# k'v for two heads as one whole-array matmul, and the later chunks' attention at full depth in one bank, in a fused linear-attention and two-layer-expert kernel

## The chip, the cores and the metric

The kernel runs as one launch on one core of a Trainium2 chip. The metric is the device time of that launch in microseconds (us); each kernel is run several times and the median is taken. Beside the timed runs there is one profiled execution, from which every row below comes.

## The reference

Three stages follow each other. A linear attention without softmax over 8 batches, 8 heads, 576 positions and a head width of 64; a dense two-layer network with a leaky activation over the 4608 tokens; and a second network in which each token goes to the one of 8 experts that its gate picks.

```python
kv = np.einsum('bhsd,bhse->bhde', k, v)
out = np.einsum('bhsd,bhde->bhse', q, kv)
rms = np.sqrt(np.mean(out * out, axis=-1, keepdims=True) + 1e-06)
x = out / rms * g_norm                      # transposed, then reshaped to (4608, 512)
h = x @ w_in
x = (np.maximum(h, 0.0) + alpha * np.minimum(h, 0.0)) @ w_out
e = argmax(x @ w_gate + modality_bias[modality_id])       # one expert for a token
out[mask_e] = gate * (np.maximum(x[mask_e] @ w1[e], 0.0) @ w2[e])
```

The change touches the first two lines alone: `kv`, a 64x64 matrix for each batch and head, and `out`, the product of q with it.

## The kernel before

The work falls into a start (the first chunk's attention, some 22 us), a loop over 12 chunks of 384 tokens (to about 883 us), and the experts after it. The instructions stand in the order in which the program is written; no planner moves them, and each engine takes its own in that order.

In the loop, a chunk `c` runs through 16 steps `s`. A step is `first(c, s)`, 12 matmuls of 384 columns (L372), then `second(c, s-1)`, 9 matmuls of 512 columns (L393), both on numbers that are split in a high and a low part. ScalarE (`A`, rows ACT), VectorE (`V`, DVE) and GpSimd (`G`, POOL) prepare the operands of `second` from what `first` gave (L374, L375, L379, L381), and VectorE computes the gate's dot products of the chunk before (L410). TensorE (`PE`) has 21 matmuls in a step, and beside them, at some steps, the attention of the chunk that comes next.

Heads are worked on in pairs: pair `p` of 4 stands for two heads, with k and v of both side by side in the 256 columns of a tile `kvt`: columns 0 to 63 and 64 to 127 hold k of the two heads, 128 to 191 and 192 to 255 hold v. The positions, 576 of them, are five slices of up to 128 rows.

- `kv_mm(b, p)`, at steps 3 and 7 of those chunks in which a new batch begins (two pairs each time), multiplies for each slice and each of the two heads 64 columns of k with 64 columns of v (L229). The result for head 0 lies on partitions 0 to 63, that for head 1 on 64 to 127 of a bank `kvps`, each in columns of its own.
- `kv_evict(b)` copies these two quarters into `kvbd[b % 2]`, whose other two quarters stay at zero from the start: for each pair `p` it is a 128x128 matrix with the two heads' matrices on its diagonal.
- `attend(c, ts)`, at step 8 for two tiles of 128 tokens and at step 10 for one, multiplies q with it (L246). A matmul takes 32 tokens of one head: 64 rows deep, 32 columns of weights (q is the stationary operand), 64 columns of output. The four pairs of heads go to partitions 0, 32, 64 and 96 and the two heads of a pair to two banks `ps[0]` and `ps[1]`.
- `attended(c, t)`, at steps 8, 9 and 10, copies each of the two banks into `xs` (L256) and squares each into `junk` (L257), in strides that put the heads side by side again. VectorE then sums the squares (L289).

The first batch and the first chunk don't go this way: `kv_pair` (L265) and `attend_pair` (L271) do the same product with whole-array matmuls of 128 rows, 128 columns of weights and 128 columns of output, and f32 operands as well. `warm` (L824) keeps TensorE busy at the start with transposes of a 128x128 tile.

The banks that `attend` and `kv_mm` write come from a pool of two (`ps_a`, through `other()`), so an allocation waits until the one before the last has been read. Every f32 matmul shows in the trace as two passes, each a record of a weight load (engine PEld) and one of a matmul (PE); the split matmuls of L372 and L393 show as one.

Of the kernel before, what the change touches and what calls it, by code (L numbers as in the profile page):

```python
# [15 lines left out]
AF = mybir.ActivationFunctionType  # L16
# [7 lines left out]
S = 576  # L24
E = 8
NB = 8
CT = 384
# [21 lines left out]
def fused(ctx: ExitStack, tc, qT, kv, g2, wmoe, alpha, wgate, bias, modality, w12, out):  # L49
    nc = tc.nc  # L50
    V, A, G, PE, SP = nc.vector, nc.scalar, nc.gpsimd, nc.tensor, nc.sync
# [36 lines left out]
    kvbd = [one.tile([128, 4, 128], F32, name=f"kvbd{i}") for i in range(2)]  # L88
    xs = one.tile([128, 3, D], F32, name="xs")
    xhi = one.tile([128, 4, CT], F32R, name="xhi")  # L90
    xlo = one.tile([128, 4, CT], F32R, name="xlo")
    junk = one.tile([128, D], F32, name="junk")
# [7 lines left out]
    q_t, kv_t, raw_t, cut_t, g_t, xt_t, y_t, ms_t, sp_t = {}, {}, {}, {}, {}, {}, {}, {}, {}  # L100
    lg_t, kvps, hot_t, tps_t, pos_t, sq_t, rsqrt_t, yb_t = {}, {}, {}, {}, {}, {}, {}, {}
    ops, ops_t = [], {}
# [4 lines left out]
    def other(n=512):  # L107
        return (pools[1] if pools else ps_a).tile([128, n], F32, tag="a", name="a")
# [114 lines left out]
    def kv_mm(b, p):  # L223
        if p == 0:
            kvps[b] = four(other())
        t = kv_t.pop((b, p))
        for s in range(5):
            for o in (0, 64):
                PE.matmul(kvps[b][o:o + 64, p, o:o + 64], t[:, s, o:o + 64], t[:, s, 128 + o:192 + o], start=(s == 0), stop=(s == 4))  # L229

    def kv_evict(b):
        ps = kvps.pop(b)
# [2 lines left out]

    def attend(c, ts):

        q = q_t[c]
        ps = [other(256 * len(ts)).rearrange("p (a b) -> p a b", b=64) for _ in range(2)]
        for a in range(4 * len(ts)):  # L240
            o = ts[0] * 128 + 32 * a
            kvs = kvbd[(c * CT + o) // S % 2]
            for p in range(4):
                for h in range(2):
                    r = slice(64 * h, 64 * h + 64)
                    PE.matmul(ps[h][32 * p:32 * p + 32, a, :], q[r, p, o:o + 32], kvs[r, p, r], start=True, stop=True)  # L246
        for i, t in enumerate(ts):
            ops_t[c, t] = [p[:, 4 * i:4 * i + 4, :] for p in ps]

    def attended(c, t):  # L250
        ps = ops_t.pop((c, t))
        x = xs[:, t, :].rearrange("p (a h b) -> p a h b", a=4, h=2)
        sq = junk.rearrange("p (a h b) -> p a h b", a=4, h=2)
        xt_t[c, t] = xs[:, t, :].rearrange("p (a b) -> p a b", b=64)
        for h in range(2):
            A.copy(x[:, :, h, :], ps[h])  # L256
            A.activation(sq[:, :, h, :], ps[h], AF.Square)  # L257

    def kv_pair(p):

# [537 lines left out]
    with tc.manual_schedule():  # L798
# [71 lines left out]
        for c in range(NCH):  # L870
# [3 lines left out]
            for s in range(NFB):  # L874
# [55 lines left out]
                if kvb and s in (3, 7):  # L930
                    kv_mm(kvb[0], s - 3 and 2)
                    kv_mm(kvb[0], (s - 3 and 2) + 1)
# [8 lines left out]
                if nxt < NCH:  # L941
                    at = AT if c == 0 else 8
                    if at < s <= at + 3:
                        squares(nxt, s - at - 1)
                    if at <= s < at + 3:
                        if s != at + 1:
                            attend(nxt, (0, 1) if s == at else (2,))
                        attended(nxt, s - at)
                    if s == 11 and nxt + 1 < NCH:
                        load_q(nxt + 1)  # L950
                    if c == 0 and s in (at + 4, at + 5):
                        rsqrt(nxt, later, s - at - 4)
                    if c == 0 and s == at + 5:
                        scale_x(nxt, 0)
                    if c == 0 and s == at + 6:
                        scale_x(nxt, 1)
                        turn_x(nxt, 0)
                        scale_x(nxt, 2)
                        turn_x(nxt, 1)
                        turn_x(nxt, 2)  # L960
                    if c > 0 and s == at + 3:
                        rsqrt(nxt)
                    if c > 0 and s == at + 4:
                        scale_x(nxt, 0)
                        scale_x(nxt, 1)
                        turn_x(nxt, 0)
                    if c > 0 and s == at + 5:
                        scale_x(nxt, 2)
                        turn_x(nxt, 1)
                        turn_x(nxt, 2)  # L970
# [34 lines left out]
        c = NCH - 1  # L1005
# [109 lines left out]
```

## Time and profile before

| what | us |
|---|---|
| median of 3 runs | 1352.28 (1351.08 to 1353.52) |
| the profiled execution's own time | 1351.64 |
| its span, first to last instruction | 1350.0 |
| PE busy | 1335.8 (99%) |
| PEld busy | 1149.8 (85%) |
| DVE busy | 978.3 (72%) |
| POOL busy | 643.9 (48%) |
| ACT busy | 606.6 (45%) |

The profiled execution is 0.64 us below the median of the runs. Busy times are sums over the whole span, in which records of one engine that overlap count once. A matmul's record lasts longer than the time until the next one may begin, so what one costs is read from start to start. The granted clock of TensorE is at its full level (2.4 GHz) in all 40 slices of the page.

### The profile page before, as it was taken

Reading aid. Unit: us, or ns where it says so; the run is one execution under the profiler, and the core shown is the slowest. Engines: PE = TensorE matmul, PEld = TensorE weight load, DVE = VectorE, ACT = ScalarE, POOL = GpSimd, SP = SyncE. Lnnn points to the kernel's source line nnn. Section 1 sums busy time; section 2 is a strip of 40 time slices with the busy share of each in tenths; the row PEclk is TensorE's granted clock in tenths of the full one; section 3 lists DMA queues with packets and bytes.
Section 4 is the critical chain, followed back from the end, with each engine's and each line's share of the span. In section 5 each row is a group of like instructions: output and inputs, shape, how many; then the busy total and the mean of one; then the engine's idle time right before and its main releaser. Section 6 shows DMA issues by size and latency. Waiting matters only on the chain. (4 is left out here: it accounts for less than half of the span.)

```text
span 1350.0 us, 26562 instructions
## 1 busy us (share of the span) xinstructions
PE 1335.8 (99%) x8856; PEld 1149.8 (85%) x8856; DVE 978.3 (72%) x2041; ACT 606.6 (45%) x1329; POOL 643.9 (48%) x647
## 2 busy tenths in 40 slices
PE   8999999999999999999999999999999999999997
PEld 7888888889888889888888988878888888888886
DVE  5779686877877686969596969576766666666664
ACT  4763443443434343443434343254544444444444
POOL 4866464554645454645464555453333333333321
PEclk9999999999999999999999999999999999999999
DMA  8956556452646463546564443557411271637784
GB/s 302 325 191 198 200 195 205 166 195 100 206 153 209 161 207 128 180 166 216 167 212 153 141 165 126 202 189 264 150 48 47 63 279 48 265 102 294 302 320 187
DMA packets 84340, 250.68 MB, mean 186 GB/s; under 512 B 13101, under 2 KB 34605, under 8 KB 82032
## 3 DMA queue, kind: packets, MB, share of 16 engines
q1 hardware_dynamic: 72448, 220.82, 46.1%
q0 software_dynamic: 11760, 28.14, 6.4%
q8 instruction: 78, 1.28, 0.4%
q14 instruction: 54, 0.44, 0.1%
HBM read 158.69 MB, written 91.54 MB: 185 GB/s over the span
## 5 line engine op out<-in xcount | busy, mean ns | idle before, releaser
L372 PE MATMUL h<-xhi,W 128*128 128x384 f32 x1536 | 428.8, 341 | 0.2 <-POOL W L186 0.2
L381 POOL TENSOR_TENSOR glo<-gg,ghi 128x384 fp32r<-128x384 f32 x192 | 202.9, 1057 | 365.7 <-ACT ghi L379 321.4
L410 DVE CUSTOM_DVE_ANT_0 junk<-yrow,wg_sb 128x512 f32<-128x512 f32 x242 | 305.9, 1264 | 9.5 <-ACT yrow L404 4.0
L393 PE MATMUL y<-W,ghi 128*128 128x512 f32 x1152 | 299.7, 395 | 1.4 <-ACT ghi L379 1.0
L372 PEld LDWEIGHTS h<-xhi,W 128*128 128x128 f32 x1536 | 280.4, 188 | 9.9 <-POOL W L186 0.5
L372 PE MATMUL h<-xlo,W 128*128 128x384 f32 x768 | 257.9, 337 | 0.0
L393 PEld LDWEIGHTS y<-W,ghi 128*128 128x128 f32 x1152 | 212.6, 188 | 44.0 <-ACT ghi L379 9.4
L375 DVE SCALAR_TENSOR_TENSOR gg<-gg,less,h 128x384 f32<-128x384 f32 x192 | 116.9, 609 | 134.3 <-ACT gg L374 133.2
L374 ACT ACTIVATE gg<-h 128x384 f32<-128x384 f32 x192 | 94.4, 492 | 260.1 <-PE h L372 248.6
L216 POOL TENSOR_TENSOR raw<-raw 128x512 f32<-128x512 f32 x128 | 207.2, 1619 | 0.0
L651 PE MATMUL y<-W,hth 128*128 (+1 forms) x656 | 204.5, 393 | 2.0 <-DMA W<-wsp 2.0
L651 PE MATMUL h<-W,xhi 128*128 (+1 forms) x656 | 206.3, 395 | 0.0
L379 ACT CAST ghi<-gg 128x384 fp32r<-128x384 f32 x192 | 98.7, 514 | 209.2 <-DVE gg L375 209.2
L759 POOL DMA_INDIRECT out_dram<-kvbd,tail x41 | 43.4, 1058 | 279.2 <-ACT kvbd L757 238.3
L393 PE MATMUL y<-W,glo 128*128 128x512 f32 x576 | 163.4, 392 | 0.0
L372 PEld LDWEIGHTS h<-xlo,W 128*128 128x128 f32 x768 | 144.3, 188 | 6.0 <-DVE xlo L360 0.2
L651 PEld LDWEIGHTS h<-W,xhi 128*128 128x128 f32 x656 | 122.9, 188 | 29.9
L651 PEld LDWEIGHTS y<-W,hth 128*128 128x128 f32 x656 | 123.0, 188 | 28.9 <-DVE lg L410 2.4
L705 DVE TENSOR_SCALAR hh<-h 32x256 f32<-32x256 f32 (+1 forms) x320 | 129.1, 403 | 9.3 <-PE h L651 4.4
L651 PE MATMUL h<-W,xlo 128*128 (+1 forms) x328 | 129.3, 394 | 0.0
L705 ACT ACTIVATE hh<-h 32x256 f32<-32x256 f32 (+1 forms) x320 | 117.1, 366 | 25.6 <-PE h L651 21.4
L393 PEld LDWEIGHTS y<-W,glo 128*128 128x128 f32 x576 | 107.9, 188 | 23.3 <-POOL glo L381 0.8
(204 smaller groups left out, 1413.9 us busy)
## 6 DMA issues: line engine op xcount, KB each, us to landing
wsp<-raw SPq DMA_DIRECT2D x128, 512.0 KB, 3.0
W<-wsp SPq DMA_DIRECT2D x16, 4096.0 KB, 13.7
raw<-in_w_dram SPq DMA_DIRECT2D x128, 256.0 KB, 3.3
kvt<-in_kv_dram SPq DMA_DIRECT2D x30, 512.0 KB, 6.3
xs<-xb POOLq DMA_DIRECT2D x140, 64.0 KB, 2.5
raw<-in_wmoe_dram SPq DMA_DIRECT2D x17, 511.8 KB, 5.8
qT<-in_qT_dram SPq DMA_DIRECT2D x11, 768.0 KB, 8.0
wg_sb<-in_wmoe_dram SPq DMA_DIRECT2D x15, 511.8 KB, 5.3
```

What stands on the lines that cost most here:

```text
L216: G.tensor_tensor(lo, lo, hi, ALU.subtract)
L372: PE.matmul(ps, w_at(fb, part)[:, k * 128:(k + 1) * 128], x[:, k, :], start=(i == 0), stop=(i == 11))
L374: A.activation(gg, ps, AF.Relu, scale=-1.0)
L375: V.scalar_tensor_tensor(gg, gg, less[:, fb:fb + 1], ps, ALU.mult, ALU.add)
L379: A.copy(ghi, gg)
L381: G.tensor_tensor(glo, gg, ghi.bitcast(F32), ALU.subtract)
L393: PE.matmul(y_t[c][t], a[:, t * 128:(t + 1) * 128], w, start=(fb == i == 0), stop=(fb == NFB - 1 and i == 2))
L410: V.tensor_tensor_reduce(spare if i >= 22 else junk, y, wg_sb[:, e, :], 1.0, 0.0, ALU.mult, ALU.add, lg_t[c][:, t, e:e + 1])
L651: m = PE.matmul(ps, a, w, start=start, stop=stop)
L705: m = V.tensor_scalar(to, of, 0.0, None, ALU.max) if mine else A.activation(to, of, AF.Relu)
L759: d = G.indirect_dma_start(out=out, out_offset=IndirectOffsetOnAxis(ap=tail[:, i, 1:2].bitcast(I32), axis=0), in_=y, in_offset=None, bound ...
```

## The change

`kv_mm` multiplies, for each slice, all 128 columns of k with all 128 columns of v in one matmul. The two quarters that `kv_evict` copies are the same as before; the other two hold products of one head's k with the other's v, and nothing reads them. `attend` multiplies all 128 rows of q, both heads, with the whole 128x128 matrix of the pair: the zeros off the diagonal keep the heads apart, the output is 128 columns wide, and one bank holds a tile of 128 tokens. `attended` copies and squares that bank at once.

```diff
     def kv_mm(b, p):
...
         for s in range(5):
-            for o in (0, 64):
-                PE.matmul(kvps[b][o:o + 64, p, o:o + 64], t[:, s, o:o + 64], t[:, s, 128 + o:192 + o], start=(s == 0), stop=(s == 4))
+            PE.matmul(kvps[b][:, p, :], t[:, s, 0:128], t[:, s, 128:256], start=(s == 0), stop=(s == 4))
...
     def attend(c, ts):
-        q = q_t[c]
-        ps = [other(256 * len(ts)).rearrange("p (a b) -> p a b", b=64) for _ in range(2)]
-        for a in range(4 * len(ts)):
-            o = ts[0] * 128 + 32 * a
-            kvs = kvbd[(c * CT + o) // S % 2]
-            for p in range(4):
-                for h in range(2):
-                    r = slice(64 * h, 64 * h + 64)
-                    PE.matmul(ps[h][32 * p:32 * p + 32, a, :], q[r, p, o:o + 32], kvs[r, p, r], start=True, stop=True)
-        for i, t in enumerate(ts):
-            ops_t[c, t] = [p[:, 4 * i:4 * i + 4, :] for p in ps]
+        for t in ts:
+            ps = other()
+            for a in range(4):
+                o = t * 128 + 32 * a
+                kvs = kvbd[(c * CT + o) // S % 2]
+                for p in range(4):
+                    PE.matmul(ps[32 * p:32 * p + 32, a * 128:a * 128 + 128], q_t[c][:, p, o:o + 32], kvs[:, p, :], start=True, stop=True)
+            ops_t[c, t] = ps
...
     def attended(c, t):
         ps = ops_t.pop((c, t))
-        x = xs[:, t, :].rearrange("p (a h b) -> p a h b", a=4, h=2)
-        sq = junk.rearrange("p (a h b) -> p a h b", a=4, h=2)
         xt_t[c, t] = xs[:, t, :].rearrange("p (a b) -> p a b", b=64)
-        for h in range(2):
-            A.copy(x[:, :, h, :], ps[h])
-            A.activation(sq[:, :, h, :], ps[h], AF.Square)
+        A.copy(xs[:, t, :], ps)
+        A.activation(junk, ps, AF.Square)
```

On TensorE, at steps 7 and 8 of the first chunk (L229 is k'v and L246 the attention of two tiles; the numbers are the output's partitions and columns, `kvbd_100` and `kvbd_101` the two matrices), before:

```order
L393 MATMUL y<-W,glo 128x512 x3
L229 MATMUL a<-kvt 64x64 x20
L372 MATMUL h<-xhi,W 128x384
...
L393 MATMUL y<-W,ghi 128x512 x6
L393 MATMUL y<-W,glo 128x512 x3
L246 MATMUL a<-kvbd_100,qT 32x64 x48
L246 MATMUL a<-kvbd_101,qT 32x64 x16
L372 MATMUL h<-xhi,W 128x384
```

and with the change, where the lines have moved by one to seven:

```order
L386 MATMUL y<-W,glo 128x512 x3
L228 MATMUL a<-kvt 128x128 x10
L365 MATMUL h<-xhi,W 128x384
...
L386 MATMUL y<-W,ghi 128x512 x6
L386 MATMUL y<-W,glo 128x512 x3
L243 MATMUL a<-kvbd_100,qT 32x128 x24
L243 MATMUL a<-kvbd_101,qT 32x128 x8
L365 MATMUL h<-xhi,W 128x384
```

Nothing changes its place among the other matmuls; there are half as many of either kind, of twice the output's columns. On ScalarE, at step 8 of the first chunk (L256 and L257 are the copy and the square, L374 and L379 belong to `first`), before:

```order
L256 COPY xs<-a 128x4x64
L257 ACTIVATE junk<-a 128x4x64
L256 COPY xs<-a 128x4x64
L257 ACTIVATE junk<-a 128x4x64
L185 CAST W<-yrow_90 128x512
L374 ACTIVATE gg<-h 128x384
L379 CAST ghi<-gg 128x384
```

and with the change:

```order
L249 COPY xs<-a 128x512
L250 ACTIVATE junk<-a 128x512
L185 CAST W<-yrow_90 128x512
L367 ACTIVATE gg<-h 128x384
L372 CAST ghi<-gg 128x384
```

Four instructions of 256 elements a partition have become two of 512, in the same place.

## Rows read from the trace of the kernel before

**Rows 1.** Table by stage, later chunks: PE busy, PEld, DVE, ACT, POOL (x instructions).

```profile
135.00:880.00 745.00, 744.14 (x5821) 661.27 (x5806) 561.28 (x1189) 299.07 (x660) 397.26 (x320) 1.00 0.51 175
```

**Rows 2.** Waits of TensorE's matmuls, the first row: us in total, times, longest.

```profile
PE y L651 <- DMA W<-wsp: 2.0, 1, 2.0
```

**Rows 3.** Timeline of PE: start us, us, line, tiles; a k'v visit, then none.

```profile
181.78 0.85 PE L393 MATMUL y<-W,glo 128*128 128x512 f32 x3
182.56 1.39 PE L229 MATMUL a<-kvt 128*64 128x64 f32 x40
...
184.32 0.51 PE L372 MATMUL h<-xhi,W 128*128 128x384 f32 x2
...
187.46 0.85 PE L393 MATMUL y<-W,glo 128*128 128x512 f32 x3
188.15 0.34 PE L372 MATMUL h<-xhi,W 128*128 128x384 f32 x1
...
188.50 0.51 PE L372 MATMUL h<-xhi,W 128*128 128x384 f32 x2
```

**Rows 4.** Timeline of PE: the attention of two tiles, then of one.

```profile
205.62 0.85 PE L393 MATMUL y<-W,glo 128*128 128x512 f32 x3
206.40 1.49 PE L246 MATMUL a<-kvbd,qT 64*32 64x64 f32 x128
...
208.27 0.51 PE L372 MATMUL h<-xhi,W 128*128 128x384 f32 x2
...
215.74 0.85 PE L393 MATMUL y<-W,glo 128*128 128x512 f32 x3
216.52 0.86 PE L246 MATMUL a<-kvbd,qT 64*32 64x64 f32 x64
...
217.76 0.51 PE L372 MATMUL h<-xhi,W 128*128 128x384 f32 x2
```

**Rows 5.** Lines L229 and L246: passes in all, ns min/median/max, first and last start.

```profile
L229 PE MATMUL a<-kvt x560: 221/222/270, 39.7 to 705.2; 128*64 128x64 f32 x187
L246 PE MATMUL a<-kvbd,qT x2112: 212/216/241, 63.6 to 790.2; 64*32 64x64 f32 x192
```

**Rows 6.** Timeline of PE: whole-array f32 matmuls at the start, back to back.

```profile
15.10 0.61 PE L271 MATMUL a<-kvbd,qT 128*128 128x128 f32 x4
15.54 0.39 PE L271 MATMUL spare<-kvbd,qT 128*128 128x128 f32 x2
15.77 4.75 PE L824 MATMUL h<-ident 128*128 128x128 f32 x42
```

**Rows 7.** Lines L265, L372 and L393, columns as in rows 5.

```profile
L265 PE MATMUL kvp<-kvt x20: 272/275/377, 5.1 to 9.0; 128*128 128x128 f32 x16, 64*128 64x128 f32 x4
...
L372 PE MATMUL h<-xhi,W x1536: 333/336/445, 22.8 to 878.8; 128*128 128x384 f32 x192
...
L393 PE MATMUL y<-W,ghi x1152: 387/394/506, 27.5 to 882.3; 128*128 128x512 f32 x192
```

**Rows 8.** L246 by stretch: PE busy (passes touching it), PEld, clock, DMA share, GB/s.

```profile
206.39:206.47 0.08, 0.07 (x8) 0.07 (x15) 1.00 0.84 307
206.47:206.53 0.06, 0.06 (x16) 0.06 (x24) 1.00 1.05 410
206.53:206.59 0.06, 0.06 (x24) 0.06 (x26) 1.00 1.05 410
```

**Rows 9.** L229 by stretch: the first row without PEld, the others as rows 8.

```profile
182.65:183.23 0.58, 0.58 (x22) 1.00 0.79 325
...
182.55:182.65 0.10, 0.09 (x2) 0.09 (x4) 1.00 0.57 164
182.65:182.71 0.06, 0.06 (x4) 0.06 (x6) 1.00 0.00 0
```

**Rows 10.** ScalarE's copies and squares of a bank, ns in the middle place.

```profile
L256 ACT COPY xs<-a x66: 345/373/382, 66.9 to 791.0; 128x256 f32<-128x256 f32 x66
...
L404 ACT COPY yrow<-y x36: 577/592/609, 100.2 to 892.0; 128x512 f32<-128x512 f32 x36
```

## The prediction

> **What bounds the kernel.** The page has PE busy for 99% of the span, so I read the table by stage first: PE is busy for 744.14 of the 745 us in which the later chunks run, while DVE has 561, POOL 397 and ACT 299 [rows 1]. PE is the bound in that stage and has no gap that another engine could fill or lose. The waits say the same: the longest single wait of a matmul in the whole run is 2.0 us, in the experts, where this change has nothing [rows 2]. So an engine other than PE matters here only if it comes late, and each microsecond that PE's queue grows or shrinks by goes into the span. A busy PE doesn't tell what a matmul costs, though, since a record lasts longer than the time to the next. I therefore read visits in the timeline: from the start of the three L393 matmuls ahead to the third L372 matmul behind, and the same stretch where nothing lies between.
>
> **What the visits cost now.** With nothing between, the stretch takes 188.50 - 187.46 = 1.04 us; with a visit to k'v (40 passes) 184.32 - 181.78 = 2.54 us [rows 3]. A k'v visit costs 1.50 us, and there are 560/40 = 14 of them [rows 5]. The attention of two tiles (128 passes) takes 208.27 - 205.62 = 2.65 us and so costs 1.61 us, that of one tile (64 passes) 217.76 - 215.74 = 2.02 us and so 0.98 us [rows 4]. A chunk has one of each, 192 passes, and 2112/192 = 11 chunks have them [rows 5]. All in all 14 x 1.50 + 11 x 2.59 = 49.5 us of PE stand under the change.
>
> **What sets a pass's price.** This is where the forecast is decided. Passes in different column or row tiles of the array go side by side; passes in one tile follow each other. In k'v, two passes (one for each head) go together, and ten such pairs take 0.58 us: 22 passes touch that stretch, two of which began ahead of it, so 58 ns a pair [rows 9]. In the attention eight passes go together, eight new ones in each 0.06 us of the visit's beginning (8, 16, 24 touch the stretches, and none has ended yet) [rows 8]. Both have 64 output columns, but 64 and 32 columns of weights: the price of a group is the same, so it is not the weights that set it. It is the output columns: f32 records grow from 222 ns (64 columns) to 275 (128), 53 ns for 64 columns more, which is two cycles of 2.4 GHz a column [rows 5, 7], while the split matmuls of L372 and L393 grow from 336 to 394, 58 ns for 128 columns more [rows 7]. The ends of records are modelled, so I take from them only that f32 runs at about half the rate. The price that I use is read from starts: six passes of the whole array, 128 columns wide, f32, take 15.77 - 15.10 = 0.67 us [rows 6], 112 ns each (0.1117), nearly twice 58.
>
> **k'v.** L265 is the same operation, operands and type as the new matmul. A visit has 10 matmuls, 20 passes, none of which can go beside another since each fills the array: 20 x 0.1117 = 2.23 us. The old 20 pairs took 20 x 0.058 = 1.16 us, so of the 1.50 some 0.33 us were spent on the way in and out: the first k'v pass starts 0.78 us after the L393 row where L372 would have started after 0.69 [rows 3], and the rest is the way back. This stays with column tiles. In rows 6 the array changes from one whole-array kind of matmul to the next within the same 0.67 us, so I take none of it for the new visit. Hence 2.23 - 1.50 = +0.73 us a visit, 14 x 0.73 = **+10.2 us**. If the way in and out stayed, it would be 14 x 0.33 = 4.6 us more.
>
> **Attention.** A tile of tokens has now 16 matmuls, 32 passes, that go in four column tiles: 8 groups of four, each 128 columns wide. If the four go side by side, as the four pairs of heads did before, a group costs the same 0.112 us: 16 groups are 1.79 us, 8 are 0.89. The way in and out remains, and I take the 0.33 us of k'v for it. Two tiles cost 1.79 + 0.33 = 2.12 instead of 1.61 us, one costs 0.89 + 0.33 = 1.22 instead of 0.98: 0.51 + 0.24 = +0.75 us a chunk, 11 x 0.75 = **+8.2 us**. The old attention had as much array time for 16 groups of eight at 0.06, about 0.96 us for two tiles, and was slower than that behind its first groups: 128 passes from 206.40 take till the L372 behind [rows 4], more than the groups explain, which half as many passes will not suffer from. That loss is already inside the 1.61, so the sum takes it as saved.
>
> **ScalarE.** Four instructions a tile, 2 x 373 ns for the copies and about as much for the squares, become two of the size of L404's copy, 592 ns [rows 10]: 0.3 us less for each of 33 tiles, some 10 us of ACT in all. PE covers it, being busy all through the stage [rows 1]; nothing is gained, and as ACT does less, nothing comes late if that cover were gone. A tile's bank is now free after its own two reads instead of the two banks together after eight, so the second visit, at step 10, finds its bank earlier than before. The zeros and the unread quarters of the banks add no instruction.
>
> **The sum.** +10.2 + 8.2 = +18.4 us on the profiled 1351.64 us, 1370.1; the median of the runs is 0.64 us above that execution, so **1370.7 us**. With p for the price of a group of 128 columns, all of it is 14 x (20p - 1.50) + 11 x (24p + 0.66 - 2.59) = 544p - 42.2 us: the change breaks even at p = 78 ns, and the rows give 112.
>
> **Rivals.**
> 1. *The column tiles run at the split matmuls' rate*, 58 ns for 128 columns [rows 7]: the attention then costs 16 x 0.058 + 0.33 = 1.26 and 0.79 us, 0.54 us less a chunk, -5.9 us, while k'v keeps its measured 112 ns as the price of loading 128 columns of weights. Sum +4.3, 1356.6 us. For it: weights could be what sets 112. Against it: 32 and 64 columns of weights gave one price [rows 8, 9]. The Trainium skill ("TensorE: Matmul & The Clock Gate", Back-to-back issue gap) gives N/2.4 + 2.5 ns from one matmul of N columns to the next at 2.4 GHz. As an estimate from that page a group of 128 columns would take 56 ns, and the sum would be that of this rival; the f32 passes of rows 6 take twice that, so the trace does not agree. Chance 6%.
> 2. *Not slower*: the 112 ns belong to the start, where loads from memory fill the DMA engines, and the same pass costs 58 ns in the loop. Then k'v costs 20 x 0.058 = 1.16, 0.34 less a visit, -4.8 us; with -5.9 from the attention 1341.6 us. It decides below p = 78 ns. Against it: k'v's groups take the same 0.06 us at a DMA share of 0.00 as over ten pairs at 0.79 [rows 9]. Chance 3%.
> 3. *Weight loads show*: with full depth all tiles use the same 128 rows, and a group's loads no longer lie under the group ahead. In the attention the first group takes 0.08 us where the next take 0.06 [rows 8], so a load that shows costs about 0.02 us: 24 groups x 11 x 0.02 = 5.3 us more, 1376 us; at 0.03, 1378.6. Against it: k'v is full depth too, and its first pair alone takes 0.10 us, the next 0.06 [rows 9]. The Trainium skill (same page, The mechanism, on packing small matmuls) says that a load goes under running matmuls only where the row groups differ. By that rule this rival would be the likeliest; the k'v pairs of rows 9 contradict it. Chance 8%.
> 4. *Four full-depth tiles don't go side by side* but two by two, as k'v has shown at most: 24 x 11 x 0.112 = 29.6 us more, 1400 us. Against it: eight went together before [rows 8]. Chance 3%.
>
> **The numbers.** The forecast has 80%. Its own range is 1366 to 1374: k'v's way in and out may stay (+4.6, half of it likely), and the attention's may be shorter than 0.33 us (0.1 us x 22 = -2.2). Rival 3 lies above it, up to 1378.6; the range of 1364 to 1378 takes in nearly all of both and leaves out rivals 1, 2 and 4, 12%, and the edges. About 0.2%, 2.7 us, is what a measurement of this kernel can tell from no change. Slower by more: forecast, rivals 3 and 4 and most of rival 1, 94%; within: the rest of rival 1 and a p near 78 ns, 3%; faster: rival 2, 3%.
>
> **What would show it.** Right: 280 passes of L228 and 1056 of L243; a k'v visit from L386 to the third L365 in about 3.27 us, the attention in 3.16 and 2.26; the passes of k'v 112 ns apart, those of the attention four within a few ns and then a pause to 112; about 18 us more in the stage of the chunks and none in the experts. Wrong: k'v's passes 58 ns apart, or the groups of four 58 (rivals 2 and 1), 130 or more (3), or 220 (4) apart, or a wait of PE for ACT or DVE around the visits.

## The result and the profile after

| kernel | median, us | runs |
|---|---|---|
| before | 1352.28 | 1351.08 to 1353.52, 5 runs |
| changed | 1368.11 | 1367.54 to 1369.19, 5 runs |

The changed kernel is slower: the ratio is 1.0124, with a 95% interval of 1.0112 to 1.0135, which is 15.1 to 18.3 us. Forecast were 1370.7 us and +18.4. The two profiled executions took 1351.64 and 1368.92 us, with spans of 1350.0 and 1367.3.

Where the 17.3 us between the spans came from is read from the busy times by stage: the start, the first chunk of the loop, chunks 2 to 11, the last chunk, the experts. The columns are the stretch, its length, then the busy times of PE, PEld, DVE, ACT and POOL, the granted clock, the DMA share and GB/s. First the kernel before:

```profile
0.00:22.78 22.78, 18.98 (x137) 16.96 (x137) 10.01 (x35) 7.04 (x14) 8.63 (x32) 1.00 0.91 320
22.78:100.19 77.41, 76.67 (x624) 66.35 (x622) 62.42 (x110) 57.19 (x114) 56.70 (x49) 1.00 0.74 259
100.19:815.71 715.52, 715.52 (x5782) 636.86 (x5781) 549.77 (x1146) 293.32 (x648) 387.94 (x310) 1.00 0.52 176
815.71:882.95 67.24, 66.38 (x326) 57.96 (x325) 47.06 (x100) 21.00 (x46) 33.36 (x27) 1.00 0.47 169
882.95:1350.00 467.05, 458.28 (x1996) 371.64 (x1994) 309.00 (x651) 228.07 (x513) 157.30 (x229) 1.00 0.50 184
```

and the changed one:

```profile
0.00:23.53 23.53, 19.01 (x137) 16.99 (x137) 10.02 (x35) 7.04 (x14) 8.62 (x32) 1.00 0.94 317
23.53:102.48 78.95, 78.37 (x487) 68.96 (x486) 62.52 (x110) 56.94 (x108) 56.64 (x49) 1.00 0.72 251
102.48:832.98 730.50, 730.50 (x4582) 654.09 (x4581) 548.51 (x1146) 290.03 (x588) 387.71 (x310) 1.00 0.51 172
832.98:900.22 67.24, 66.38 (x326) 57.95 (x325) 47.10 (x100) 21.06 (x46) 33.38 (x27) 1.00 0.47 169
900.22:1367.30 467.08, 458.30 (x1996) 371.53 (x1994) 308.82 (x651) 228.03 (x513) 157.23 (x229) 1.00 0.50 184
```

The first chunk is 1.54 us longer and the ten behind it 14.98; the last chunk and the experts are the same to 0.1 us. The remaining 0.75 us lie in the start, which has the same instructions in both kernels. PE is busy for the whole of the ten chunks, before as after, so it was TensorE's own work that grew. ACT's busy time fell by 3.3 us there, and the time doesn't show it.

The same stretches of PE as in [rows 3, 4], now of the changed kernel (start, length of the group): a k'v visit, a stretch with no visit, the attention of two tiles and that of one.

```profile
184.78 0.85 PE L386 MATMUL y<-W,glo 128*128 128x512 f32 x3
185.46 2.39 PE L228 MATMUL a<-kvt 128*128 128x128 f32 x20
...
188.04 0.52 PE L365 MATMUL h<-xhi,W 128*128 128x384 f32 x2
...
191.18 0.85 PE L386 MATMUL y<-W,glo 128*128 128x512 f32 x3
...
192.21 0.51 PE L365 MATMUL h<-xhi,W 128*128 128x384 f32 x2
...
210.06 0.85 PE L386 MATMUL y<-W,glo 128*128 128x512 f32 x3
210.83 1.95 PE L243 MATMUL a<-kvbd,qT 128*32 128x128 f32 x64
...
213.17 0.51 PE L365 MATMUL h<-xhi,W 128*128 128x384 f32 x2
...
220.62 0.85 PE L386 MATMUL y<-W,glo 128*128 128x512 f32 x3
221.40 1.08 PE L243 MATMUL a<-kvbd,qT 128*32 128x128 f32 x32
...
222.87 0.51 PE L365 MATMUL h<-xhi,W 128*128 128x384 f32 x2
```

Without a visit the stretch is 1.03 us, as before. A visit costs what its stretch has above 1.04:

| visit | before | forecast | after | visits |
|---|---|---|---|---|
| k'v, two pairs of heads | 1.50 | 2.23 | 188.04 - 184.78 - 1.04 = 2.22 | 14 |
| attention, two tiles | 1.61 | 2.12 | 213.17 - 210.06 - 1.04 = 2.07 | 11 |
| attention, one tile | 0.98 | 1.22 | 222.87 - 220.62 - 1.04 = 1.21 | 11 |

That is 14 x 0.72 + 11 x (0.46 + 0.23) = 10.1 + 7.6 = 17.7 us at the visits; the rows above stand for all of them, since the visits of a kind differ by less than 0.01 us in each of the two traces. Of the 17.7 us, 16.5 show in the loop (1.54 + 14.98). The other 1.2 us were taken from small waits that the kernel before had between its visits. The largest stands in its first chunk, where a group of PE rows ends an idle time (in brackets: us, and what ended it); the changed kernel has no such row at that step:

```profile
89.43 1.66 PE L393 MATMUL y<-W,ghi 128*128 128x512 f32 x6 [0.17 <-ACT ghi L379]
```

From the three L393 matmuls ahead of it to the three behind (86.32 to 90.92) this step takes 4.60 us; in the changed kernel, between the same matmuls (now L386, 89.06 to 93.22), it takes 4.16. Of the 1.2 us, 0.6 lie in the first chunk and 0.6 in the ten behind it, where PE's busy time shows no gap: a record lasts longer than the time to the next start, and a shorter wait hides in that.

The single passes, in stretches of 0.11 us that each begin where a group begins (PE busy and the passes that touch the stretch); first three of k'v, L228, then three of the attention, L243:

```profile
185.45:185.57 0.12, 0.11 (x1) 1.00 0.00 0
185.57:185.68 0.11, 0.11 (x2) 1.00 0.00 0
185.68:185.79 0.11, 0.11 (x3) 1.00 0.64 261
...
210.83:210.95 0.12, 0.12 (x4) 1.00 0.00 0
210.95:211.06 0.11, 0.11 (x8) 1.00 0.00 0
211.06:211.17 0.11, 0.11 (x12) 1.00 0.00 0
```

k'v takes a new pass each 0.11 us and the attention four new ones together, so the four column tiles do go side by side, and a group costs a little under the 0.112 us of the forecast: (2.07 - 0.33)/16 = 0.109 us. The granted clock is 1.00 in all six stretches and the DMA share 0.00 in five of them, so neither sets the price.

Line by line (passes, ns min/median/max, first and last start), the two kinds of matmul:

```profile
L228 PE MATMUL a<-kvt x280: 271/275/275, 40.4 to 721.2; 128*128 128x128 f32 x140
...
L243 PE MATMUL a<-kvbd,qT x1056: 272/273/297, 65.8 to 807.5; 128*32 128x128 f32 x176
```

Half as many passes of either kind, as the order said [rows 5], each with the record length of a 128-column f32 matmul [rows 7].

### The profile page after: what moved, and what is told of

Its sections match the earlier page's. It is cut to its first block, busy times and chain, and to the rows that moved or that the text cites. A ratio compares the mean times of both kernels' runs of the same rounds, so it can differ in the third digit from the quotient of the medians.

```text
span 1367.3 us, 23802 instructions
## 1 busy us (share of the span) xinstructions
PE 1352.6 (99%) x7520; PEld 1169.5 (86%) x7520; DVE 977.0 (71%) x2041; ACT 603.1 (44%) x1263; POOL 643.6 (47%) x647
## 5 line engine op out<-in xcount | busy, mean ns | idle before, releaser
L374 POOL TENSOR_TENSOR glo<-gg,ghi 128x384 fp32r<-128x384 f32 x192 | 202.7, 1056 | 382.9 <-ACT ghi L372 331.9
L403 DVE CUSTOM_DVE_ANT_0 junk<-yrow,wg_sb 128x512 f32<-128x512 f32 x242 | 302.8, 1251 | 9.5 <-ACT yrow L397 4.0
L386 PE MATMUL y<-W,ghi 128*128 128x512 f32 x1152 | 299.3, 395 | 1.2 <-ACT ghi L372 0.9
L386 PEld LDWEIGHTS y<-W,ghi 128*128 128x128 f32 x1152 | 212.7, 188 | 43.2 <-ACT ghi L372 8.6
L372 ACT CAST ghi<-gg 128x384 fp32r<-128x384 f32 x192 | 98.7, 514 | 203.1 <-DVE gg L368 203.1
L386 PE MATMUL y<-W,glo 128*128 128x512 f32 x576 | 163.4, 392 | 0.0
L386 PEld LDWEIGHTS y<-W,glo 128*128 128x128 f32 x576 | 107.9, 188 | 23.4 <-POOL glo L374 0.8
```

What stands on the lines that cost most here:

```text
L372: A.copy(ghi, gg)
L374: G.tensor_tensor(glo, gg, ghi.bitcast(F32), ALU.subtract)
L386: PE.matmul(y_t[c][t], a[:, t * 128:(t + 1) * 128], w, start=(fb == i == 0), stop=(fb == NFB - 1 and i == 2))
L403: V.tensor_tensor_reduce(spare if i >= 22 else junk, y, wg_sb[:, e, :], 1.0, 0.0, ALU.mult, ALU.add, lg_t[c][:, t, e:e + 1])
```

## The experiments

The theory: an f32 pass costs what its output columns cost, 58 ns for 64 and 110 to 112 for 128; passes in different tiles share that; a visit in tiles pays 0.33 us more for the way in and out, a whole-array visit nothing. The rivals say that it is the pass or its weight load that costs, that the two halves of the change share a cost, or that the way in and out is no fixed price. In each timeline below, the visit runs from the first row to the last, and 1.04 us of it are the stretch without a visit. The kernel before took 1353.40 us (median of 9 runs) beside the first four experiments, 1355.60 us in its one run beside the next three, and 1352.68 us (14 runs) beside the last. Five of the experiments ran once; of them the visits are what counts, and a difference of some microseconds between totals says little.

**Each half alone.** The first kernel has the new `kv_mm` and the old attention, the second the old `kv_mm` and the new attention.

```diff
# e1_kv_alone, against the kernel before
-            for o in (0, 64):
-                PE.matmul(kvps[b][o:o + 64, p, o:o + 64], t[:, s, o:o + 64], t[:, s, 128 + o:192 + o], start=(s == 0), stop=(s == 4))
+            PE.matmul(kvps[b][:, p, :], t[:, s, 0:128], t[:, s, 128:256], start=(s == 0), stop=(s == 4))
# e2_att_alone: the rest of the change, without these lines
```

> The change to k'v alone, the attention as before. Theory (a whole-array f32 pass of 128 columns costs 0.112 us, and a whole-array visit has no way in and out): 14 visits at 2.24 us instead of 1.51, +10.2 us on the kernel before, about 1362.5 us, and the attention's visits stay at 1.62 and 0.99 us. Rival (the whole loss of some 16 us is the attention's, and k'v only moved): within 3 us of before.

> The change to the attention alone, k'v as before. Theory (groups of four tiles, 0.110 us a group of 128 columns, 0.33 us for the way in and out): 2.08 and 1.21 us instead of 1.62 and 0.99, 0.68 us a chunk, 11 chunks, +7.5 us on the kernel before, about 1359.8 us; with the run before it the two parts add up to the whole change. Rival (the two parts share a cost, such as a switch between tilings): the two runs add up to over 20 us or under 14.

k'v alone took 1360.76 us against 1353.40 for the kernel before beside it, a ratio of 1.0061 (1.0047 to 1.0074); the attention alone 1359.93, 1.0049 (1.0035 to 1.0063). PE's timeline of a k'v visit of the one, and of a two-tile visit of the other:

```profile
182.57 0.85 PE L392 MATMUL y<-W,glo 128*128 128x512 f32 x3
183.26 2.39 PE L228 MATMUL a<-kvt 128*128 128x128 f32 x20
...
185.84 0.51 PE L371 MATMUL h<-xhi,W 128*128 128x384 f32 x2
```

```profile
207.60 0.85 PE L387 MATMUL y<-W,glo 128*128 128x512 f32 x3
208.38 1.95 PE L244 MATMUL a<-kvbd,qT 128*32 128x128 f32 x64
...
210.72 0.51 PE L366 MATMUL h<-xhi,W 128*128 128x384 f32 x2
```

The visits cost 2.23 and 2.08 us, as in the changed kernel. The ratios give +8.3 us (6.4 to 10.0) and +6.6 us (4.7 to 8.5), together 14.9, where the medians of the whole change have 15.8. The loop, which holds all visits, is read more closely; its rows for the two kernels, columns as in the tables by stage:

```profile
22.64:892.38 869.74, 868.30 (x6448) 776.11 (x6447) 655.73 (x1356) 372.65 (x804) 477.72 (x386) 1.00 0.53 181
23.94:891.35 867.41, 865.43 (x5672) 766.18 (x5671) 660.60 (x1356) 367.89 (x737) 477.98 (x386) 1.00 0.53 181
```

It took 860.17 us before and 876.69 in the changed kernel. The halves make it 9.6 and 7.2 us longer, together 16.8, and the whole change 16.5. So the halves add up. k'v alone came out 1 to 2 us below its 10.2 by ratio and span, just beyond the interval of the ratio, although its visits are as long as expected. In the loop 0.6 us are missing, which went into waits that were there before; the rest lies outside the loop, where nothing was changed. The rival that leaves k'v within 3 us of before has fallen. A shared cost, which would bring the sum under 14 or over 20, is ruled out by the visits and the loops, and not by the ratios alone, whose sum of 14.9 has some 3 us of noise.

**Output columns or passes.** The changed kernel with each attention matmul split in two of 64 output columns.

```diff
-                for p in range(4):
-                    PE.matmul(ps[32 * p:32 * p + 32, a * 128:a * 128 + 128], q_t[c][:, p, o:o + 32], kvs[:, p, :], start=True, stop=True)
+                for h in range(2):
+                    for p in range(4):
+                        PE.matmul(ps[32 * p:32 * p + 32, a * 128 + 64 * h:a * 128 + 64 * h + 64], q_t[c][:, p, o:o + 32], kvs[:, p, 64 * h:64 * h + 64], start=True, stop=True)
```

> The changed kernel with each attention matmul of 128 output columns split in two of 64 (same 128 rows, same 32 columns of weights): twice as many passes and weight loads. Theory (output columns set a group's price): 32 groups of four at 0.058 us, 1.86 + 0.33 = 2.19 us for two tiles and 1.26 for one, 0.2 us a chunk more than the changed kernel, +1.8 us, about 1370 us. Rival (each pass costs its price whatever its columns, 0.11 us a group): 3.85 and 2.09 us, +29 us, about 1397 us.

```profile
209.62 0.85 PE L387 MATMUL y<-W,glo 128*128 128x512 f32 x3
210.40 2.00 PE L244 MATMUL a<-kvbd,qT 128*32 128x64 f32 x128
...
212.78 0.51 PE L366 MATMUL h<-xhi,W 128*128 128x384 f32 x2
```

Twice the passes and twice the weight loads, in 3.16 us instead of 3.11; the run took 1368.68 us. The visit costs 2.12 us (2.19 expected), and a group of 64 columns (2.12 - 0.33)/32 = 0.056 us. The columns set the price; the pass and its load of 32 columns cost next to nothing. It also shows that full depth as such doesn't keep loads from going under running matmuls: 64 loads more cost 0.05 us. The Trainium skill ("TensorE: Matmul & The Clock Gate", The mechanism) has a rule by which a load overlaps running matmuls only where the row groups differ; here all four tiles use all rows, and the trace differs from that rule. The same section also names a background weight buffer as a way for a load to go ahead, which would agree with the trace; no run here tells which way the loads took.

**What a load of 128 columns costs, and what 64 with all of v.** Two ways to split k'v: all 128 columns of weights with 64 output columns, and two column tiles of 64 columns of weights with 128 output columns each.

```diff
# e4_kv_loads, against the changed kernel
-        for s in range(5):
-            PE.matmul(kvps[b][:, p, :], t[:, s, 0:128], t[:, s, 128:256], start=(s == 0), stop=(s == 4))
+        for o in (0, 64):
+            for s in range(5):
+                PE.matmul(kvps[b][:, p, o:o + 64], t[:, s, 0:128], t[:, s, 128 + o:192 + o], start=(s == 0), stop=(s == 4))
# e5_kv_cols, against the changed kernel
-            PE.matmul(kvps[b][:, p, :], t[:, s, 0:128], t[:, s, 128:256], start=(s == 0), stop=(s == 4))
+            for o in (0, 64):
+                PE.matmul(kvps[b][o:o + 64, p, :], t[:, s, o:o + 64], t[:, s, 128:256], start=(s == 0), stop=(s == 4))
```

> The changed kernel with each k'v matmul split in two of 64 output columns, each with all 128 columns of weights: 40 passes a visit, each a load of 128 columns and 64 columns out. If output columns alone set the price: 40 x 0.058 = 2.32 us a visit, +1.2 us on the changed kernel, about 1369 us. If a load of 128 columns cannot be had under 0.11 us either (the first L372 behind a visit now starts its second matmul 0.28 us after the first instead of 0.17, a load that shows): 40 x 0.112 = 4.47 us, +31 us, about 1399 us. I expect the second.

> The changed kernel with k'v in two column tiles again (64 columns of weights each, side by side) but all 128 columns of v for both: 40 passes a visit in 20 pairs. Theory (output columns set the price, tiles bring the way in and out): 20 x 0.112 + 0.33 = 2.57 us a visit, 0.33 more than the changed kernel, +4.6 us, about 1372.7 us. Rival (weight loads set it, 64 columns are half the price): 1.16 + 0.33 = 1.49 us a visit, about 1357.6 us.

```profile
189.01 0.85 PE L387 MATMUL y<-W,glo 128*128 128x512 f32 x3
189.70 4.57 PE L229 MATMUL a<-kvt 128*128 128x64 f32 x40
...
194.52 0.51 PE L366 MATMUL h<-xhi,W 128*128 128x384 f32 x2
```

```profile
184.78 0.85 PE L387 MATMUL y<-W,glo 128*128 128x512 f32 x3
185.56 2.40 PE L229 MATMUL a<-kvt 128*64 128x128 f32 x40
...
188.36 0.51 PE L366 MATMUL h<-xhi,W 128*128 128x384 f32 x2
```

With whole-array loads a visit costs 194.52 - 189.01 - 1.04 = 4.47 us, 0.112 for each of the 40 passes though each has half the columns. The run took 1403.74 us, 4 to 5 us above what was expected; in its trace 2.9 of them stand in the experts (469.94 us instead of 467.08), where one matmul waits 3.2 us for VectorE, and 0.9 in the last chunk, and neither has k'v in it. With two tiles of 64 columns of weights a visit costs 2.54 us and the run took 1373.26: 20 pairs at (2.54 - 0.33)/20 = 0.11 us, where the old pairs of 64 output columns cost 0.058.

So a whole-array f32 pass costs 0.112 us with 64 output columns as with 128, and that the load of 128 columns is what holds it there is the reading that fits: the records of loads last 106 ns for 32 columns (L246), 138 for 64 (L229) and 192 for 128 (L228), 0.9 ns for each column more, which as an estimate makes some 0.115 us for 128. No run separates the load from another floor under whole-array f32 passes. By this reading either will do it: 128 f32 columns out, or 128 columns of weights in, cost 0.11 us, and the new k'v matmul has both. The sign that the expectation of the first run goes by, 0.28 us between the first two L372 matmuls behind a visit, says nothing: in the kernel before they start 0.28 us apart too (183.87 and 184.15).

**The way in and out.** The changed kernel with all three tiles of a chunk in one visit.

```diff
-            ps = other()
+            ps = ops_t[c, 0] if t == 2 else other()
...
-                        if s != at + 1:
-                            attend(nxt, (0, 1) if s == at else (2,))
+                        if s == at:
+                            attend(nxt, (0, 1, 2))
```

> The changed kernel with the attention of all three tiles in one visit at step 8; the third tile is written over the first one's bank, so the first tile's attention is lost. Theory (0.33 us a tiled visit whatever its length): 24 x 0.110 + 0.33 = 2.97 us instead of 2.08 + 1.21 = 3.29, -0.33 us a chunk, -3.6 us on the changed kernel, about 1364.5 us. Rival (the way in and out grows with what was issued, or overlaps elsewhere): no change from the changed kernel, 1368 us.

```profile
208.87 0.85 PE L386 MATMUL y<-W,glo 128*128 128x512 f32 x3
209.65 2.83 PE L243 MATMUL a<-kvbd,qT 128*32 128x128 f32 x96
...
212.87 0.51 PE L365 MATMUL h<-xhi,W 128*128 128x384 f32 x2
```

The visit costs 2.96 us instead of 2.07 + 1.21 = 3.28: 0.32 us saved a chunk, one way in and out. The one run took 1366.08 us, and its span is 2.9 us shorter than the changed kernel's, of 3.6 expected. In the trace the eleven chunks with a visit are 0.24 to 0.33 us shorter each, together 3.2; the last chunk, which has none, is 0.5 us longer, as in three of the other single runs (0.5 to 0.9), and why was not followed up. Other numbers send the tokens to other experts, so the stage of the experts can't be compared.

**Why the old attention took longer than its groups.** The kernel before with one head of each pair, whose result serves for both.

```diff
-                for h in range(2):
+                for h in range(1):
...
-            ops_t[c, t] = [p[:, 4 * i:4 * i + 4, :] for p in ps]
+            ops_t[c, t] = [ps[0][:, 4 * i:4 * i + 4, :] for _ in range(2)]
```

> The kernel before with the attention of one head of each pair alone; both halves of the output take it, so half of the attention is left out. As many groups as before, each of four passes instead of eight. If the groups set the old attention's time: 1.62 and 0.99 us as before, about 1352 us. If the old attention was late in getting its passes (its first 32 go at eight in 0.06 us, the rest slower): 16 x 0.058 + 0.33 = 1.26 us for two tiles and 0.79 for one, 0.56 us a chunk less, -6.1 us on the kernel before, about 1346 us. I expect the second.

```profile
205.34 0.85 PE L393 MATMUL y<-W,glo 128*128 128x512 f32 x3
206.12 1.10 PE L246 MATMUL a<-kvbd,qT 64*32 64x64 f32 x64
...
207.61 0.51 PE L372 MATMUL h<-xhi,W 128*128 128x384 f32 x2
```

As many groups as before, with four passes each, cost 1.23 us instead of 1.61: the groups alone do not explain the old attention, and 0.38 us of its visit are a loss that comes with the other four passes of each group. The first 24 passes come at eight in 0.06 us [rows 8]. In the starts of single passes, the first four groups of eight begin 0.06 us apart but for the way in, those behind them 0.07 to 0.08, and every fourth 0.10 to 0.15; with one head the groups of four keep 0.06 to the end. That passes come too late, and not that the second bank or the second half of the rows costs something, is argued from those first groups, which have both and lose nothing; no run shows it by itself. The run took 1347.97 us, its span 3.6 us below that of before, where the visits save 6.5. In the ten middle chunks the saving shows in full, 0.6 us each; in the first chunk it went into waits behind the visits, of the kind that the changed kernel lost. Here too the tokens go to other experts, so the visit is what counts.

**A version that beats both.** The old matmuls are the cheap ones, and what is left to save on them is the way in and out. For the six batches that begin after the first chunk, all four pairs of heads are taken in one k'v visit at step 3. The room for k and v of the third pair is q's tile, which stands empty until q is loaded behind the visit, and for the fourth `xs`, which is empty from step 15 to step 8.

```diff
# e8_kv_once, against the kernel before
+        elif once and p >= 2:
+            if p == 2:
+                h = one.tile([128, 4, CT], F32, tag="qT", name="qT").rearrange("p a b -> p (a b)")
+            else:
+                h = xs.rearrange("p a b -> p (a b)")
+            t = h[:, 0:1280].rearrange("p (s c) -> p s c", c=256)
+            V.memset(t[64:128, 4, :], 0.0)
...
+                if kvb and c > 0 and s == 0:
+                    load_kv(kvb[0], 3, True)
+                if kvb and c > 0 and s == 3:
+                    for p in range(4):
+                        kv_mm(kvb[0], p)
+                if kvb and c > 0 and s == 4:
+                    load_q(nxt)
-                if kvb and s in (3, 7):
+                if kvb and c == 0 and s in (3, 7):
...
-                if kvb and s == 7:
+                if kvb and s == (3 if c else 7):
...
-                        load_q(nxt + 1)
+                        load_kv(kvn[0], 2, True) if kvn else load_q(nxt + 1)
```

> The kernel before (k'v and attention in small tiles), with the two k'v visits of a batch made one at step 3 for the six later batches; the third pair's k and v lie in q's tile until then and the fourth's in xs, and q is loaded after the visit. Theory (0.33 us for the way in and out of each tiled visit, whatever its length): 40 x 0.058 + 0.33 = 2.67 us instead of twice 1.51, -0.34 us six times, -2.0 us on the kernel before, about 1350 us. Rival (q or the fourth pair comes late, or the zeroing of two quarters on VectorE delays a step): no gain or a loss, with a wait of TensorE for a load at step 3 or 8 in the trace.

```profile
183.06 0.85 PE L400 MATMUL y<-W,glo 128*128 128x512 f32 x3
183.84 1.39 PE L236 MATMUL a<-kvt 128*64 128x64 f32 x40
185.06 0.75 PE L236 MATMUL a<-qT 128*64 128x64 f32 x20
185.64 0.75 PE L236 MATMUL a<-xs 128*64 128x64 f32 x20
...
186.77 0.51 PE L379 MATMUL h<-xhi,W 128*128 128x384 f32 x2
```

The visit costs 186.77 - 183.06 - 1.04 = 2.67 us instead of 3.00, to the hundredth what was expected, and no matmul in it waits for a load. The median is 1349.06 us against 1352.68 of the kernel before beside it, a ratio of 0.9973 (0.9960 to 0.9985), 2.0 to 5.4 us less. The loop's row:

```profile
23.97:882.34 858.37, 856.78 (x6728) 761.18 (x6727) 653.14 (x1368) 372.48 (x804) 478.81 (x386) 1.00 0.54 183
```

The visits account for 2.0 us, and the loop is 1.8 us shorter than before's 860.17, since one of the 22 attention visits took 0.23 us longer. The span of the profiled execution is 1.5 us shorter: its start is 1.2 us longer and its experts 0.9 shorter, with the same instructions. The rest of the median's 3.6 us I cannot place.

## Why the prediction was right

The sign and the size were right: +18.4 us forecast, +15.8 measured between the medians (15.1 to 18.3), 17.3 between the spans. That the spans come so near is in part luck: the visits grew by 17.7 us, 1.2 us of it went into waits, and 0.75 us came on top from the start, which the change doesn't touch. By its steps:

- **PE as the bound.** Right but for 1.2 us. The ten middle chunks have no idle PE in either kernel by the busy time, and nearly all of each visit's growth went into the time; that there is "no gap" was read from busy times, which hide short waits. ACT got shorter for nothing, and by 3.5 us in all (606.6 to 603.1), not by some 10: the lengths of its records, which the step added up, overlap. From the first of them to the next instruction behind, the four take 1.06 us (66.89 to 67.95) and the two 0.96 (68.34 to 69.30).
- **k'v, +0.73 us a visit.** Right: +0.72, 14 visits. The price was read from six passes of L271 [rows 6], which have the shape of the new matmul throughout. L265, which the step names as the same operation, is that only in four of its five slices: its last slice has 64 rows (64*128 in [rows 7]), and ten of its passes, with nothing waited for, take 1.40 us to the next L271 (12.92 to 14.32), 0.14 each. Pass by pass, the starts are 0.11 us apart and, around the two passes of 64 rows, 0.2. The whole-array visit has no way in and out: its first pass starts 0.68 us after the L386 row, as L372 does after 0.69 in [rows 3] where nothing lies between. What the step had only by argument, that the output columns set the price and not the weights, holds for 32 and 64 columns of weights, where it was read. For the new matmul it is at most half of the truth, since a whole-array pass costs the same 0.112 us with half the output. The number was safe from that, since L271 has 128 columns on both sides too.
- **Attention, +0.75 us a chunk.** Right in kind, 0.06 too high: 0.46 + 0.23 = 0.69 us. A group of four column tiles costs 0.109 us and not the 0.112 of a whole-array pass, and there are 24 groups a chunk. The 0.33 us for the way in and out, taken over from k'v, were right.
- **The old attention's loss**, which the sum counted as saved: that there is one, 0.38 us for two tiles, is shown by the run with one head; what causes it is argued. The new attention has no such loss, with half the passes and twice the time for each group.
- **Not in the sum:** 1.2 us of waits in the loop which the longer visits took up.
- **The rivals.** The rate of the split matmuls fell with the groups at 0.11 us. The price of the start alone fell too: L228 costs 0.11 us in the loop at a DMA share of 0.00. Loads that show and tiles that go two by two fell with four new passes in each 0.11 us.

Put together: the change halves the number of matmuls, and the number was not what they cost. On the diagonal of a 128x128 matrix only half of the columns of each row carry anything; the small tiles skipped the other half and ran side by side, and the large ones stream it.

## What to carry to other kernels

Count a small f32 matmul's cost in output columns streamed per tile, at the price that a trace shows for its type, and divide by the tiles that go side by side; for the whole array put in no less than the 0.11 us that a pass cost here with 64 columns as with 128. In these runs fewer and larger matmuls lost because they streamed more columns in all. Price a way in and out of a tiled stretch as an operation of its own, 0.33 us here, and merge such stretches before reshaping what is in them. Where the same operation stands elsewhere in the program, its start-to-start time there is the best price to be had, if its shapes are the same in every slice.

## What the runs showed that was not expected

- A whole-array f32 pass costs the same 0.112 us with 64 output columns as with 128 (the split with 64: 4.47 us for 40 passes). If that is its load of 128 columns, the whole-array matmul has no slack on either side.
- With eight tiles at once, 128 passes cost 1.61 us, and 64 in as many groups of four 1.23. It looks as if TensorE ran out of passes; that is argued, not shown.
- The stage before the loop, whose instructions are the same in all kernels, took 22.78, 23.53 and 23.97 us in the profiled executions of the kernel before, the changed one and the last one. A difference of about a microsecond between two spans is therefore better read from the stage that was changed.
